# One dV quarter in front of each even unit's end product, and the gradient half first on ScalarE

## The chip, the cores and the metric

The kernel runs on one core of a Trainium2 chip. The core has five engines, each with an instruction queue of its own that is worked in order: TensorE (PE in the profile, with its weight loads shown as PEld), VectorE (DVE), ScalarE (ACT), GpSimd (POOL) and SyncE (SP, which here issues most of the DMA transfers). They meet through semaphores. TensorE writes its results to PSUM, an accumulator memory of eight banks; ScalarE and VectorE read them from there. The metric is the device time of one execution in microseconds, as the median of several runs. The profile is of one further execution.

## The reference

The kernel computes the output and all eight input gradients of two attention blocks side by side: A, a linear attention, and B, an ordinary softmax attention with 16 heads of 28 that share one key and one value head. The change is in B's main loop. Cut to that part:

```python
def _B_ref(x, wq, wk, wv, wo):          # x: 1 x 2048 x 448
    q = (x @ wq)                         # 16 heads of 28
    k, v = x @ wk, x @ wv                # one head of 28 each
    scores = einsum("bhqd,bkd->bhqk", q, k) * 28 ** -0.5
    p = softmax(scores)
    o = einsum("bhqk,bkd->bhqd", p, v)
    return o @ wo

def reference(..., grad_out):
    out, vjp = jax.vjp(f, A_x, A_wqkv, A_wo, B_x, B_wq, B_wk, B_wv, B_wo)
    return (out, *vjp(grad_out))
```

Going back through the softmax needs, for every head, query and key, the exponential of the score (E), the product of the output's gradient with the value (dP) and the product of both (dS). From these come o (from E and v), dq (from dS and k), dk (from dS and q) and dv (from E and the output's gradient).

## The kernel before

A first stage (about 185 us) does block A and prepares B: transposed q, k and v, each replicated into four groups of 32 partitions. The main loop then does B forwards and backwards, and a last stage (from about 1000 us) turns dq, dk and dv into the gradients of the weights and of x.

**Blocks and units.** The main loop runs over 64 blocks. A block is 256 queries and two heads (`blk`, L679). It is cut into 8 units, each of 256 keys: `u = 8 b + tp`, 512 units in all. A unit's work comes in stages that lie many units apart, so that one turn of the loop (L926) does, for the current u:

- scores of unit u (called S0 and S1 here, one for each of the two heads, "halves"): four matmuls, two key pieces of 128 for each half, on 32 rows of the array (`rows_SD`, L683);
- dP of unit w = u - 16 (D0 and D1), four matmuls in the same form in the same function. The four combinations use the array's four groups of 32 rows. The list `todo` (L687 to L689) gives their order;
- E of unit u on ScalarE: exp0 (L946) for half 0, exp1 (L992) for half 1, each 128 x 512;
- dS of unit w: half 0 on VectorE straight from PSUM (L958); half 1 by a copy on ScalarE (cp, L960) and a product on GpSimd (L961);
- in even units, the "end product" (`o_dq`, L889): o of units u-2 and u-1 and dq of the dS of units u-20 and u-19, 16 matmuls of 256 columns on four groups of 32 columns;
- in odd units, dk: 16 matmuls of 32 x 32 and 512 columns (`dk_m`, L860), from dS transposed by VectorE two units after dS was made (L1039);
- dv in four quarters a block (half h, query half qb; `dv_mm`, L896), each of four matmuls of 512 columns. It reads `eN`, E transposed by a DMA that SyncE issues behind exp1 of every fourth unit (L994), and `don`, the output's gradient divided by the softmax's sum. Before, the quarters stand in even units behind the end product: two when u modulo 8 is 4, one at 6, one at 2 (L1006 to L1008).

Beside these stand, once in a block: the copy of o from PSUM (L974, u modulo 8 = 1), the transposes of o (`onat_T`, L806, at 2) and its normalising (`o_norm`, L813), the copy of dq (L977, at 3), the row sums (`row_D`, at 4), the transposes of the gradient (`don_T`, L834, and `don_copy`, at 6), and from unit 32 a piece of an output projection (`do_proj`, `out_proj`, at 0; before unit 27 in odd units).

**Banks.** dP has two PSUM banks (`DB`), one for each half, used again in each unit: D0 of a unit may start when VectorE's product of the unit before has read its bank, D1 when cp of the unit before has. The scores turn over three banks (`SB`): S0 of u uses number 2u, S1 number 2u+1, modulo 3. So S1 takes the bank of S0 of the unit before, and the third, the "spare", is the bank of exp1 of the unit before and of the next unit's S0. In between it serves the transposes and projections.

**Order.** The order on each engine in the main loop is the order in which the code issues (`manual_schedule`, L917); nothing is moved by a scheduler. The lines that matter:

```python
            todo = [(0, 0), (0, 1), (1, 0), (1, 1)] * 2
            if sp is not None and dp is not None and u % 2 == 0:
                todo = [(0, 0), (0, 1), (1, 0)] * 2 + [(1, 1)] * 2
```

The first number is 0 for scores and 1 for dP, the second is the half.

Of the kernel before, what the change touches and what calls it, by code (L numbers as in the profile page):

```python
# [8 lines left out]
ACT = mybir.ActivationFunctionType  # L9
# [16 lines left out]
def kernel(  # L26
# [21 lines left out]
    nc = tc.nc  # L48
# [3 lines left out]
    scale = float(DH) ** -0.5  # L52
# [594 lines left out]
    NB = 64  # L647
# [3 lines left out]
    with ExitStack() as cs_:  # L651
# [17 lines left out]
        def eT(u):  # L669
            return ETs[u // 4 % 5][:, u % 4, :, :]  # L670

        def eN(b, c):
            return ENs[(2 * b + c // 2) % 6][:, 16 * (c % 2):16 * (c % 2) + 16, :]

        def mmt(out, lhsT, rhs, pos, start, stop):
            nc.tensor.matmul(out, lhsT=lhsT, rhs=rhs, start=start, stop=stop, tile_position=pos,  # L676
                             skip_group_check=True)

        def blk(b):  # L679
            qc, pair = divmod(b, 8)  # L680
            return qc, pair, pair // 2, pair % 2

        def rows_SD(u, sp, dp):  # L683
            b, tp = divmod(u, 8)
            w = u - 16
            qc, pair, g, hp = blk(b)
            todo = [(0, 0), (0, 1), (1, 0), (1, 1)] * 2  # L687
            if sp is not None and dp is not None and u % 2 == 0:
                todo = [(0, 0), (0, 1), (1, 0)] * 2 + [(1, 1)] * 2  # L689
            seen = {}  # L690
            for d in todo:
                if (dp if d[0] else sp) is None:
                    continue
                k, h = d
                t2 = seen.get(d, 0)
                seen[d] = 1
                t = 2 * tp + t2
                tc_ = slice(t * P, (t + 1) * P)
                oc = slice(t2 * 256, (t2 + 1) * 256)
                r = 64 * (1 - hp if k else hp) + 32 * h  # L700
                if k:
                    mmt(dp[h][:, oc], vT_rep[r:r + 32, tc_], doT[w // 8][r:r + 32, :], (r, 0), True, True)
                else:
                    mmt(sp[h][:, oc], kT_rep[r:r + 32, tc_], qT_B[g][r:r + 32, qc * 256:(qc + 1) * 256],
                        (r, 0), True, True)
# [96 lines left out]
        def due(u, lag):  # L802
            b, r = divmod(u - lag, 8)
            return b if r == 0 and 0 <= b < NB else None

        def onat_T(b, bank):  # L806
            onp = bank[:, 0:P].rearrange("p (q h c) -> p q h c", q=2, h=2)
            for qb in range(2):
                nc.tensor.transpose(onp[:, qb, :, :].rearrange("p h c -> p (h c)"), oTs[0:64, qb * P:(qb + 1) * P],  # L809
                                    identF[0:64, 0:64], tile_position=(0, 0))  # L810
            onps[b] = onp
# [48 lines left out]
        def dk_m(b, m, other=0):  # L860
            qc, pair, g, hp = blk(b)
            h, B, s = m // 8, (m // 2) % 4, m % 2
            for a in range(4):
                rhs = dsx[b][32 * a:32 * a + 32, :, h, :, :].rearrange(
                    "p u t (b i s) -> p u t b i s", b=4, s=2)[:, :, :, B, :, s]
                k = 32 * ((a + 2) % 4) if other else 32 * a
                mmt((dk_two if other else dk_acc)[k:k + 32, :],
                    qX[qc][32 * a:32 * a + 32, B, s, pair * 64 + 32 * h:pair * 64 + 32 * h + 32],
                    rhs, (32 * a, k), other == 2 or b == 0 and m == 0, other == 0 and b == NB - 1 and m == 15)
# [19 lines left out]
        def o_dq(vs, ys):  # L889
            for v, y in zip(vs, ys):  # L890
                todo = [f(i) for f, i in ((o_mm, v), (dq_mm, y)) if 0 <= i < NU]
                for _ in range(2):
                    for g_ in todo:
                        next(g_)

        def dv_mm(dv_acc, b, h, qb):  # L896
            for c in range(4):
                rhs = eN(b, c).rearrange("p (u h t q) k -> p u h t q k", u=2, h=2,
                                                       t=2)[:, :, h, :, qb, :]
                mmt(dv_acc[32 * c:32 * c + 32, :], don[b][:, qb, h, :], rhs, (0, 32 * c),  # L900
                    b == 0 and h + qb == 0, b == NB - 1 and h + qb == 2)
# [15 lines left out]
        with tc.manual_schedule():  # L917
# [8 lines left out]
            for u in range(NU + 28):  # L926
                w = u - 16
                hasS = u < NU
                hasD = 0 <= w < NU
                sp = [SB[(2 * u + h) % 3] for h in range(2)] if hasS else None  # L930
                dp = DB if hasD else None
                spare = SB[(2 * u + 2) % 3] if hasS else DB[u // 4 % 2] if u > 530 else SB[2]
                rows_SD(u, sp, dp)
                if (b := due(u, 10)) is not None:
                    onat_T(b, spare)
                if (b := due(u, 14)) is not None:
# [5 lines left out]
                    dps_ = DB[u // 2 % 2] if u < 16 else dk_acc if u < 27 else spare  # L942
                    do_proj(*dpj, dps_)

                if hasS:
                    nc.scalar.activation(out=eT(u)[:, 0, :], in_=sp[0][:, :], func=ACT.Exp, scale=scale)  # L946
                if u == 1:
                    q_shift(pn3, shifts[3], [pd_.tile([P, 2, 512], BF16, name="dsT").rearrange("p a b -> p (a b)").bitcast(F32)
                                             for _ in range(1)])
                    dv_acc = psA.tile([P, 512], F32, name="aacc")  # L950
# [3 lines left out]
                if hasD:  # L954
                    dst = pd_.tile([P, 2, 512], BF16, name="dsT")
                    dsT[w] = dst
                    ew = eT(w)
                    nc.vector.tensor_tensor(out=dst[:, 0, :], in0=dp[0][:, :], in1=ew[:, 0, :], op=ALU.mult)  # L958
                    cp = pc_.tile([P, 512], BF16, name="cp")
                    nc.scalar.activation(out=cp[:, :], in_=dp[1][:, :], func=ACT.Copy)  # L960
                    nc.gpsimd.tensor_tensor(out=dst[:, 1, :], in0=cp[:, :], in1=ew[:, 1, :], op=ALU.mult)  # L961
                gq, iq = divmod(u % 64 - 30, 8)
                qq = u // 64 + 1
                if 0 <= gq < 4 and u < 448:
# [34 lines left out]
                if u % 2:  # L999
                    b, i = divmod(u - 27, 8)  # L1000
                    if 0 <= b < NB:
                        for m in range(2 * i, 2 * i + 4):
                            dk_m(b, m, (1 + (u == 519 and m == 2 * i + 1)) * (m % 2) if 519 <= u < 537 else 0)
                else:
                    o_dq((u - 2, u - 1), (u - 20, u - 19))
                    b, n = divmod(u - 20, 8)  # L1006
                    for k in {0: (0, 1), 2: (2,), 6: (3,)}.get(n, ()) if 0 <= b < NB else ():
                        dv_mm(dv_acc, b, k // 2, k % 2)  # L1008
                y = u - 18

                if 512 <= u < 528 and u % 2 == 0:
# [10 lines left out]
                if u == 533:  # L1022
                    for c in range(4):
                        nc.scalar.activation(out=post["dkvT"][32:64, c * 512:(c + 1) * 512], in_=dv_acc[32 * c:32 * c + 32, :],
                                             func=ACT.Copy)
                if u == 536:
                    dk_sum = pd_.tile([P, 2, 512], BF16, name="dsT").rearrange("p a b -> p (a b)").bitcast(F32)
                    for c in range(2):
                        r = 64 * (1 - c)
                        nc.scalar.activation(out=dk_sum[64 * c:64 * c + 64, :], in_=dk_two[r:r + 64, :], func=ACT.Copy,  # L1030
                                             scale=scale)
# [3 lines left out]
                if 0 <= y < NU:  # L1035
                    b, tp = divmod(y, 8)
                    if tp == 0:
                        dsx[b] = px_.tile([P, 8, 2, 2, 256], BF16, name="dsx")
                    nc.vector.transpose(  # L1039
                        out=dsx[b][:, tp, :, :, :].rearrange("p h t c -> p (h t c)").bitcast(F32),  # L1040
                        in_=dsT[y][:, :, :].rearrange("p h c -> p (h c)").bitcast(F32))
# [67 lines left out]
        for c in range(4):  # L1109
            r = DC_ROWS[c]  # L1110
            ps = gen(0)
            for st in range(NS):
# [3 lines left out]
                                 func=ACT.Copy)  # L1116
# [35 lines left out]
```

## Time and profile before

| what | value |
|---|---|
| median of 3 runs | 1052.08 us (1051.96 to 1053.91) |
| the profiled execution's time | 1052.68 us |
| its span, first to last instruction | 1050.9 us |
| granted TensorE clock | 1.000 |
| busy share over the span: TensorE, VectorE, ScalarE, GpSimd | 96%, 85%, 83%, 76% |
| mean of one exp0, cp, exp1 | 612, 617, 629 ns |
| mean of one product on VectorE (L958), on GpSimd (L961) | 668, 1156 ns |
| mean of one transpose on VectorE (L1039) | 699 ns |
| median of one transfer eN<-eT on SyncE | 5376 ns, 128 of them |

Busy shares over the whole span mix the stages; the main loop's own share is read from a stretch in its middle. Instructions overlap at their ends, so the time between the starts of two ScalarE instructions is shorter than the duration of one. The end of a matmul is modelled by the profiler; its start is measured.

### The profile page before, as it was taken

The page shows a single profiled execution, that of the slowest core. Times are in us where ns is not written, and L with a number is a line of the kernel's source. Part 1 is how long each engine was busy: PE and PEld are TensorE (multiplying, and loading weights), DVE is VectorE, ACT ScalarE, POOL GpSimd, SP SyncE. Part 2 cuts the span into 40 slices and gives each one's busy share as a digit, 9 for nine tenths or more (in the row PEclk, how much of TensorE's full clock was granted, in tenths as well). Part 3 has the DMA queues.
Part 4 walks back from the last instruction along what each step waited for, and adds up shares of the span by engine and source line. Part 5 has one row for each costly group of instructions (what it writes and reads, how often), then busy time and mean ns, then how long its engine had stood idle before and what let it go on. Part 6 is the DMA issues. An engine that isn't in the chain of part 4 may idle for free.

```text
span 1050.9 us, 40033 instructions
## 1 busy us (share of the span) xinstructions
PE 1008.4 (96%) x16236; PEld 486.6 (46%) x16245; DVE 895.9 (85%) x1781; ACT 871.5 (83%) x1743; POOL 798.2 (76%) x1044
## 2 busy tenths in 40 slices
PE   9999999998999999999999999999999999999998
PEld 5555554434444444444444444444444444444444
DVE  6897500669999999999999999999999999999942
ACT  6463122589999999999999999999999999999632
POOL 8601272238888998899899989988998999888860
PEclk9999999999999999999999999999999999999999
DMA  9879999299999999999999999999999999999973
GB/s 266 150 134 192 189 222 215 42 163 202 188 196 190 188 195 198 194 193 191 197 175 195 192 202 185 204 199 184 192 194 191 194 190 193 204 186 182 220 156 87
DMA packets 689058, 195.15 MB, mean 186 GB/s; under 512 B 670408, under 2 KB 686688, under 8 KB 688872
## 3 DMA queue, kind: packets, MB, share of 16 engines
q1 hardware_dynamic: 680392, 179.97, 102.1%
q0 software_dynamic: 4544, 9.46, 3.4%
q10 hardware_dynamic: 3936, 3.16, 1.0%
q8 instruction: 127, 2.08, 0.8%
q14 instruction: 59, 0.48, 0.1%
HBM read 12.60 MB, written 10.84 MB: 22 GB/s over the span
## 4 chain that ended last, share of the span: by engine, by line
PE 44%; ACT 33%; issue 14%; DVE 6%; POOL 2%; DMA 0%; ACTq 0%; DVEq 0%; POOLq 0%
ACT cp L960 17%; ACT eT L992 13%; PE agen L81 13%; PE aacc L676 10%; PE agen L676 10%; PE aacc L81 6%; ACT eT L946 2%; DVE dsT L958 2%; PE aacc L809 2%; DVE dsx L1039 2%; PE aacc L840 1%; POOL dsT L961 1%; DMA out_dram<-dsT 0%; PE agen L313 0%; PE agen L227 0%
## 5 line engine op out<-in xcount | busy, mean ns | idle before, releaser
L961 POOL TENSOR_TENSOR dsT<-cp,eT 128x512 bf16<-128x512 bf16 x512 | 587.7, 1156 | 78.9 <-ACT cp L960 73.2
L1039 DVE STREAM_TRANSPOSE dsx<-dsT 128x512 f32<-128x512 f32 x512 | 357.8, 699 | 2.8 <-POOL dsT L961 0.7
L676 PEld LDWEIGHTS <-R 32*128 32x128 bf16 (+1 forms) x9104 | 228.5, 94 | 275.0 <-issue 239.4
L958 DVE TENSOR_TENSOR dsT<-agen,eT 128x512 bf16<-128x512 f32 x512 | 341.9, 668 | 10.6 <-PE agen L676 5.4
L960 ACT ACTIVATE cp<-agen 128x512 bf16<-128x512 f32 x512 | 315.8, 617 | 11.5 <-PE agen L676 10.5
L946 ACT ACTIVATE eT<-aacc 128x512 bf16<-128x512 f32 x512 | 313.6, 612 | 13.6 <-PE aacc L676 4.3
L992 ACT ACTIVATE eT<-aacc 128x512 bf16<-128x512 f32 x512 | 322.2, 629 | 0.0
L676 PE MATMUL agen<-dsx,qX 32*32 32x512 bf16 x4024 | 264.0, 376 | 0.0
L676 PE MATMUL agen<-doT,R 32*128 32x256 bf16 x2048 | 246.7, 269 | 4.2 <-DVE dsT L958 2.5
L676 PE MATMUL aacc<-R,R 32*128 32x256 bf16 (+1 forms) x2240 | 218.5, 269 | 7.1 <-DVE oTs L819 2.0
L676 PE MATMUL agen<-eT,R 128*32 128x256 bf16 x2048 | 157.4, 274 | 0.1
L676 PE MATMUL agen<-dsT,R 128*32 128x256 bf16 x2048 | 156.6, 274 | 0.1
L676 PEld LDWEIGHTS <-qX 32*32 32x32 bf16 x4096 | 78.2, 89 | 111.7 <-issue 53.3
L676 PE MATMUL aacc<-eN,don 128*32 128x512 bf16 x1024 | 96.7, 379 | 0.0
L81 PEld LDWEIGHTS <-R 128*128 128x128 bf16 x517 | 40.9, 98 | 42.2 <-issue 12.0
L81 PE MATMUL agen<-R,R 128*128 128x448 bf16 (+1 forms) x174 | 41.1, 360 | 1.8 <-ACT R L229 0.8
L851 POOL COPY qst<-R 128x512 bf16<-128x512 bf16 x56 | 34.2, 611 | 2.9 <-DMA qX<-qst 2.8
L823 POOL TENSOR_TENSOR prod<-R,oTs 128x128 f32<-128x128 bf16 x64 | 27.6, 431 | 9.3 <-DVE oTs L819 9.3
L676 PEld LDWEIGHTS <-don 128*32 128x32 bf16 x1024 | 33.8, 97 | 0.5
L586 DVE TENSOR_TENSOR osb<-R 32x512 bf16<-32x512 bf16 x4 | 1.7, 413 | 34.7 <-ACT R L583 34.7
L262 POOL TENSOR_SCALAR wdq<-wdq 128x448 bf16<-128x448 bf16 x16 | 21.1, 1327 | 12.9 <-DVE phiT L243 12.9
L427 POOL COPY pk<-R 128x256 bf16<-128x256 bf16 x4 | 1.6, 399 | 37.7 <-DVE R L389 37.7
(234 smaller groups left out, 983.1 us busy)
## 6 DMA issues: line engine op xcount, KB each, us to landing
eN<-eT SPq DMA_TRANSPOSE x128
xa<-in_A_x_dram SPq DMA_DIRECT2D x8, 224.0 KB
ga<-in_grad_out_dram SPq DMA_DIRECT2D x4, 448.0 KB
out_dram<-osb ACTq DMA_DIRECT2D x16, 112.0 KB
xa<-in_grad_out_dram POOLq DMA_DIRECT2D x4, 448.0 KB, 9.4
out_dram<-wdq POOLq DMA_DIRECT2D x8, 224.0 KB, 5.8
eT<-in_grad_out_dram SPq DMA_DIRECT2D x4, 448.0 KB
eT<-in_B_x_dram SPq DMA_DIRECT2D x4, 448.0 KB
```

What stands on the lines that cost most here:

```text
L81: nc.tensor.matmul(out_ap, lhsT=lhsT, rhs=rhs, start=start, stop=stop, tile_position=(0, 0))
L262: nc.gpsimd.tensor_scalar(out=wq_n[:, st, 0:D], in0=wq_n[:, st, 0:D], scalar1=1.0, scalar2=None, op0=ALU.min)
L676: nc.tensor.matmul(out, lhsT=lhsT, rhs=rhs, start=start, stop=stop, tile_position=pos, skip_group_check=True)
L809: nc.tensor.transpose(onp[:, qb, :, :].rearrange("p h c -> p (h c)"), oTs[0:64, qb * P:(qb + 1) * P], identF[0:64, 0:64], tile_position=(0 ...
L823: nc.gpsimd.tensor_tensor(out=prod[b][:], in0=dnv, in1=os_, op=ALU.mult)
L851: eng.tensor_copy(out=st.rearrange("p (b s) a j -> p b s a j", s=2)[:, :, s, :, :], in_=src.unsqueeze(2).to_broadcast([P, 4, 4, 32]))
L946: nc.scalar.activation(out=eT(u)[:, 0, :], in_=sp[0][:, :], func=ACT.Exp, scale=scale)
L958: nc.vector.tensor_tensor(out=dst[:, 0, :], in0=dp[0][:, :], in1=ew[:, 0, :], op=ALU.mult)
L960: nc.scalar.activation(out=cp[:, :], in_=dp[1][:, :], func=ACT.Copy)
L961: nc.gpsimd.tensor_tensor(out=dst[:, 1, :], in0=cp[:, :], in1=ew[:, 1, :], op=ALU.mult)
L992: nc.scalar.activation(out=eT(u)[:, 1, :], in_=sp[1][:, :], func=ACT.Exp, scale=scale)
L1039: nc.vector.transpose(out=dsx[b][:, tp, :, :, :].rearrange("p h t c -> p (h t c)").bitcast(F32), in_=dsT[y][:, :, :].rearrange("p h c -> p ...
```

## The change

Three things are moved; nothing is added or taken away.

1. The order of the eight matmuls of scores and dP becomes the same in every unit: D1, D0, S0, twice, then S1 twice.
2. On ScalarE, cp comes first in a unit, then exp0, then exp1 (before: exp0, cp, exp1).
3. Each even unit issues one dV quarter, just behind the scores and dP and in front of the transposes, the projections and the end product. A block's quarters come at units 18, 20, 22 and 24 after the block's first, in the order (0,0), (0,1), (1,0), (1,1) of half and query half; before, they came at 20 (two), 22 and 26, behind the end product.

```diff
-            todo = [(0, 0), (0, 1), (1, 0), (1, 1)] * 2
-            if sp is not None and dp is not None and u % 2 == 0:
-                todo = [(0, 0), (0, 1), (1, 0)] * 2 + [(1, 1)] * 2
+            todo = [(1, 1), (1, 0), (0, 0)] * 2 + [(0, 1)] * 2
...
                 rows_SD(u, sp, dp)
+                if u % 2 == 0:
+                    b, n = divmod(u - 18, 8)
+                    if 0 <= b < NB:
+                        dv_mm(dv_acc, b, n // 4, n // 2 % 2)
                 if (b := due(u, 10)) is not None:
                     onat_T(b, spare)
...
-                if hasS:
-                    nc.scalar.activation(out=eT(u)[:, 0, :], in_=sp[0][:, :], func=ACT.Exp, scale=scale)
...
                     cp = pc_.tile([P, 512], BF16, name="cp")
                     nc.scalar.activation(out=cp[:, :], in_=dp[1][:, :], func=ACT.Copy)
                     nc.gpsimd.tensor_tensor(out=dst[:, 1, :], in0=cp[:, :], in1=ew[:, 1, :], op=ALU.mult)
+                if hasS:
+                    nc.scalar.activation(out=eT(u)[:, 0, :], in_=sp[0][:, :], func=ACT.Exp, scale=scale)
...
                     o_dq((u - 2, u - 1), (u - 20, u - 19))
-                    b, n = divmod(u - 20, 8)
-                    for k in {0: (0, 1), 2: (2,), 6: (3,)}.get(n, ()) if 0 <= b < NB else ():
-                        dv_mm(dv_acc, b, k // 2, k % 2)
```

## The prediction

> **What bounds the kernel now.** I read the busy time by stretch first, then the chain of waits, then the timelines of ScalarE, TensorE, VectorE and SyncE around 602 to 611 us, where the main loop runs evenly.
>
> ```profile
> core 0: us, PE busy (x) PEld busy (x) DVE busy (x) ACT busy (x) POOL busy (x), PEclk, DMA share, GB/s
> 600.00:700.00 100.00, 96.68 (x1902) 45.30 (x1892) 97.93 (x191) 99.15 (x201) 90.25 (x110) 1.00 1.20 194
> ```
>
> Three engines are nearly full, ScalarE (ACT) most. 201 ScalarE instructions in 100 us are 67 units of three, so a unit takes 1.49 to 1.50 us.
>
> ```profile
> PE 44%; ACT 33%; issue 14%; DVE 6%; POOL 2%; DMA 0%; ACTq 0%; DVEq 0%; POOLq 0%
> ACT cp L960 17%; ACT eT L992 13%; PE agen L81 13%; PE aacc L676 10%; PE agen L676 10%; PE aacc L81 6%; ACT eT L946 2%; DVE dsT L958 2%; PE aacc L809 2%; DVE dsx L1039 2%; PE aacc L840 1%; POOL dsT L961 1%; DMA out_dram<-dsT 0%; PE agen L313 0%; PE agen L227 0%
> ```
>
> The chain alternates between the gradient copy (cp, L960), the second exponential (exp1, L992) and TensorE. So it is a loop between ScalarE and TensorE, seen here on ScalarE over two units:
>
> ```profile
> 603.04 0.60 ACT L960 ACTIVATE cp<-agen 128x512 bf16<-128x512 f32 x1
> 603.52 0.62 ACT L992 ACTIVATE eT<-aacc 128x512 bf16<-128x512 f32 x1
> 603.99 0.63 ACT L946 ACTIVATE eT<-aacc 128x512 bf16<-128x512 f32 x1
> 604.47 0.65 ACT L960 ACTIVATE cp<-agen 128x512 bf16<-128x512 f32 x1
> 604.95 0.66 ACT L992 ACTIVATE eT<-aacc 128x512 bf16<-128x512 f32 x1
> 605.49 0.61 ACT L946 ACTIVATE eT<-aacc 128x512 bf16<-128x512 f32 x1
> ```
>
> Without a wait, starts are 1.91/4 = 0.478 us apart, so three need 1.434. The last step took 0.54, because the first exponential (exp0, L946) waited. The same stretch on TensorE:
>
> ```profile
> 604.55 0.39 PE L676 MATMUL aacc<-R,R 32*128 32x256 bf16 x2
> 604.73 0.26 PE L676 MATMUL agen<-doT,R 32*128 32x256 bf16 x1
> 605.17 0.26 PE L676 MATMUL agen<-doT,R 32*128 32x256 bf16 x1 [0.18 <-ACT cp L960]
> 605.17 0.28 PE L676 MATMUL aacc<-R,R 32*128 32x256 bf16 x2
> 605.18 0.36 PE L676 MATMUL agen<-doT,R 32*128 32x256 bf16 x2
> 605.47 1.04 PE L676 MATMUL agen<-dsx,qX 32*32 32x512 bf16 x16
> 606.45 0.28 PE L676 MATMUL aacc<-R,R 32*128 32x256 bf16 x2
> ```
>
> In an odd unit gradient half 1 (D1) stands fourth. It writes the bank that cp of the unit before must have read: cp began at 604.47, D1 at 605.17, 0.70 later. Behind D1 stand the second score pieces, and exp0 began 0.32 after the release. My tally of ScalarE's timeline over units 264 to 447, as mean times from one exp0 to the next by unit modulo 8: 1.50, 1.45, 1.70, 1.45, 1.53, 1.45, 1.51, 1.45, or 12.03 us a block of eight. The lost time lies in the steps that start at an even unit; the 1.70 is the block with the output transposes.
>
> **The change, part by part.** No engine gets or loses an instruction, so the sum is one of waits.
>
> ScalarE order cp, exp0, exp1; D1 first on TensorE. Let cp(even) begin at 0. It frees D1(odd) at 0.70, long before cp(odd), which is due at 1.43. TensorE must start the odd unit's first D1 by 1.43 - 0.43 = 1.00: the second D1 stands 0.12 behind (rows 603.51 and 603.63) and a matmul reaches ScalarE 0.31 after its start (605.17 to 605.49). So that wait goes. What is late next is S1, now last: it needs the bank of the even unit's exp0, which begins at 0.48, so S1 begins at 0.48 + 0.70 = 1.18. The dK product is queued behind it, 0.30 later (605.17 to 605.47), and takes 0.98 to the next scores (605.47 to 606.45); then D1 to cp 0.43. The loop from cp to cp over two units: 1.18 + 0.30 + 0.98 + 0.43 = 2.89. ScalarE alone needs 2 x 1.434 = 2.87. I take 2.88, against 2.94 now for the plainest pair (602.55 to 605.49).
>
> dV quarter in front of the end product. Four column tiles take 0.22 (598.46: eight last 0.60; 601.72 alike: four last 0.38). The total of four a block is unchanged. The place is new: before, the output transposes (L809), gradient transposes (L840) and projections wait behind the scores for the bank of exp1 of the unit before (21.5 us before L809 alone from 300 to 950 us). With S1(even) released at 1.18 - 1.43 = -0.25, the scores end about 0.05; exp1, begun at -0.48, frees its bank at 0.22. The dV quarter fills 0.05 to 0.27, so it costs nothing there; without that cover it would cost 4 x 0.22 = 0.88 a block. Plain pair: 0.27 + 0.55 (end product, 604.00 to 604.55) = 0.82, before the 1.00 allowed. Projection, 0.19 more: 1.01, just in time. Output transposes: the next tile shape begins 0.32 after the last dV quarter starts (second four of the eight at 598.68, scores at 599.00), then 0.26 (607.13 to 607.39), then 0.55: scores from 1.18. VectorE's normalising must also leave the spare bank, about 1.27 by its rows (0.19 + 0.29 + 0.05 after the transposes, which land near 0.74). Then the second D1 is at 1.28, cp(odd) at 1.59, dK at 1.69, and the pair takes 1.69 + 0.98 + 0.43 = 3.10, against 1.70 + 1.45 = 3.15.
>
> Block: 3 x 2.88 + 3.10 = 11.74, against 12.03; 0.29 x 60 blocks (units 32 to 511) = 17.4 us gained.
>
> Ramp, units 0 to 15, scores only: S0, S0, S1, S1 in place of alternating pairs. Two pieces of one half start 0.11 apart (603.63 and its successors), so up to 0.1 a unit on a TensorE that there sets the pace: 0 to +1.6, I take +1.5. Tail, units 512 on, gradient halves only, alternating as before: 0.
>
> SyncE's transposes eN<-eT. They are issued as before, after exp1, but their queue is close behind:
>
> ```profile
> 647.30 11.28 SPq L994 DMA_TRANSPOSE eN<-eT  x2
> 658.63 1.30 SPq L855 DMA_TRANSPOSE qX<-qst  x1
> 660.04 10.66 SPq L994 DMA_TRANSPOSE eN<-eT  x2
> ```
>
> Where a block also moves qX, the queue needs 12.6 us for eight units (647.30 to 660.04 is 12.74, the next 12.50); elsewhere 10.8 (seven eN in 37.38). Over 128 units, with the 3.4 us transpose of the outputs (599.28), that is 8 x 12.6 + 8 x 10.8 + 3.5 = 190.7, or 1.49 a unit; the new pace is 11.74/8 = 1.468. So the queue falls behind 0.022 x 416 = 9 us by unit 448. Now 10 units, not 12, lie between the last transpose of a block and the first dV that reads it: 14.7 - 5.4 (one eN) - 2.1 (the landing of eN's other transfers) = 7.2 of lag are free, and about 3 are in use. 9 - 4 = 5 us would be given back; blocks that find the queue idle have shorter transposes (4.9 against 5.4), so I take 3, between 0 and 9.
>
> Sum: -17.4 + 1.5 + 3 = -13 on the span of 1050.9, which is 1052.7 for that execution; it lies 0.6 above the median, within 0.1%. So 1039.8; I say 1040. Bounds: ScalarE never waiting in the plain pairs and no lag paid, about 1030; half the gain per block and 9 us of lag, 1052.
>
> **The rivals.**
>
> A. SyncE's queue sets the pace from early on. For: it is back to back through every qX stretch. Against: it had 7 us of lag to spare before dV needs it. 416 units at 1.49 in place of the 627 us that they take now: -7; last eight blocks -2.3, ramp +1.5: 1045.
>
> B. Slower: VectorE's product (L958) holds TensorE. D0 is second in line now, and it needs the bank that this product reads; behind D0 stand both scores, the second D1 and with it cp.
>
> ```profile
> 607.09 0.65 DVE L958 TENSOR_TENSOR dsT<-agen,eT 128x512 bf16<-128x512 f32 x1
> 610.46 0.69 DVE L958 TENSOR_TENSOR dsT<-agen,eT 128x512 bf16<-128x512 f32 x1
> ```
>
> For: the pair with the normalising costs VectorE 3.37 here against 3.10 for the rest. The others need 2.97, 2.63 and 2.62 by their rows (product to product 1.22 a unit, 0.2 to 0.33 an extra), 11.6 of 11.74 in all. Today a D0 already waits (0.28 behind its score, 599.00 to 599.30). Against: D0 may come 1.09 after cp(even) (1.43 - 0.31 - 0.03) and the next cp is still on time; the product begins near 0.05, frees the bank 0.70 later, and with a lag of 0.34 (3.37 + 0.07 for its wait on the transposes, less 3.10) that is 1.09. If the 0.34 of lag and one such 0.28 are paid each block: 12.36, +20 us: 1073. It decides from 0.29 a block.
>
> C. TensorE's own work sets the pace, and S1, last and alone, makes it longer: an undisturbed four-wide odd phase takes 0.33 (608.21 to 608.54), the new order 0.43, 0.40 a block; with 0.1 for one more change of tile shape and less 0.24 for even units (0.49 now, 603.51 to 604.00) that is +0.26 x 60 = +16: 1068. For: 96.7% busy. Against: matmul ends are modelled, and TensorE stands still 0.44 between 604.73 and 605.17. The Trainium skill ("TensorE: Matmul & The Clock Gate", section "Why this matters for your kernels") speaks for this rival: small-K matmuls gain by running concurrently in distinct row groups, and the new order takes S1 out of that company. The trace agrees on the form (four starts within 0.02 us), which alone doesn't say that TensorE sets the pace.
>
> D. The change moves the wait from exp0 to exp1 or cp and nothing is gained: 1052.
>
> **How the numbers follow.** Forecast 0.56 (its own range 1030 to 1047), A 0.2, D 0.08, B 0.12, C 0.04. The time is the forecast's, 1040. Down to 1030 and up to 1053 leaves out B and C and a little at either end, near 2 in 10. About 0.2%, 2 us, is what a measurement here can tell from no change. Faster: 0.56 + 0.2 = 0.76; same 0.08; slower 0.16.
>
> **What would show it.** Right: exp1 to cp and cp to exp0 near 0.48 in nearly every unit, steps from even units near 1.44 but for the one with output transposes; S1 in odd units starting right after exp0 ends; the wait before L809 gone; SyncE's transposes back to back with a growing lag after each exp1. Wrong: D0 waiting for L958 with cp late behind it (B), TensorE without any wait on ScalarE (C), dV waiting on a transfer (A), steps of 1.50 and above at even units.

## The result, and the profile after

The changed kernel is slower: median 1059.47 us over four runs (1058.11 to 1059.88) against 1052.99 before (1051.96 to 1054.50), a ratio of 1.0059 [1.0046, 1.0071]. Its profiled execution took 1059.88 us with a span of 1058.2, 7.3 more than before. The forecast of 1040 and its whole range were missed.

The busy time in the same even stretch of the main loop (columns as in the prediction):

```profile
core 0: us, PE busy (x) PEld busy (x) DVE busy (x) ACT busy (x) POOL busy (x), PEclk, DMA share, GB/s
600.00:700.00 100.00, 98.22 (x1875) 44.67 (x1875) 96.87 (x188) 98.03 (x198) 89.86 (x110) 1.00 1.22 196
```

ScalarE does 198 instructions in this stretch, not 201, and TensorE is the fuller by 1.5 points. TensorE has no more work than before, and it starts fewer matmuls in this stretch (1875, not 1902). So the busy time counted for one matmul grew, and not the work. The chain of waits says what stands in the way:

```profile
PE 62%; DVE 23%; POOL 6%; issue 4%; ACT 3%; DMA 1%; DVEq 0%; ACTq 0%; POOLq 0%
PE agen L676 30%; PE agen L81 13%; PE aacc L676 11%; DVE dsT L958 9%; DVE dsx L1038 8%; PE aacc L81 6%; POOL dsT L961 3%; ACT cp L960 2%; DVE R L979 1%; POOL prod L821 1%; POOL don L824 1%; DVE oTs L817 1%; DVE oTs L976 1%; POOL R L825 1%; DVE rl L816 1%
```

ScalarE fell from 33% of the chain to 3%, so the change did what it says: the wait of the first exponential behind a held D1 is gone. VectorE rose from 6% to 23%, with its product (L958) and its transpose (L1038, L1039 before) at the front. The waits for one instruction between 300 and 900 us (total us, times, longest) show the same from TensorE's side:

```profile
PEld aacc L807 <- ACT eT L994: 11.1, 49, 0.2
PE agen L676 <- DVE dsT L958: 6.3, 25, 0.3
```

The wait in front of the output transposes fell from 19.9 to 11.1 us in that window; the dV quarter fills it, for it is 19.9 again in e1 below, where the quarter is back in its old place. The wait of D0 for VectorE's product is new; before, no such line of L676 stands there. The profile names it 25 times in these 50 blocks. This is how it looks in the timeline, over units 4 and 5 of a block and then from unit 7 to unit 0 of the next:

```profile
601.76 0.62 ACT L960 ACTIVATE cp<-agen 128x512 bf16<-128x512 f32 x1
...
602.30 0.69 DVE L958 TENSOR_TENSOR dsT<-agen,eT 128x512 bf16<-128x512 f32 x1
...
602.52 0.28 PE L676 MATMUL agen<-doT,R 32*128 32x256 bf16 x1
...
603.04 0.26 PE L676 MATMUL agen<-doT,R 32*128 32x256 bf16 x1 [0.25 <-DVE dsT L958]
...
603.05 0.28 PE L676 MATMUL agen<-doT,R 32*128 32x256 bf16 x1
...
603.43 0.60 ACT L960 ACTIVATE cp<-agen 128x512 bf16<-128x512 f32 x1
...
607.27 0.68 ACT L994 ACTIVATE eT<-aacc 128x512 bf16<-128x512 f32 x1
...
607.44 0.27 PE L676 MATMUL agen<-doT,R 32*128 32x256 bf16 x2
...
607.81 0.63 ACT L960 ACTIVATE cp<-agen 128x512 bf16<-128x512 f32 x1
```

First part: the product starts 0.54 after cp. D1 starts at 602.52, D0 stands second and can't start before 603.04, 0.74 after the product's start; the second D1 and so the next cp come behind it. The step from cp to cp is 1.67, not 1.43. Second part: a plain pair. The second D1 starts at 607.44 and cp at 607.81, 0.37 later; exp1 had begun at 607.27, so a free ScalarE would have taken cp at 607.75.

My tally of ScalarE's timeline says where the whole difference lies. It gives the mean time from the first ScalarE instruction of a unit to that of the next, for units 144 to 447, by unit modulo 8, in us:

| pair of units | before | predicted | after | after less predicted |
|---|---|---|---|---|
| 0, 1 (plain) | 2.947 | 2.88 | 2.956 | 0.08 |
| 2, 3 (output transposes, normalising) | 3.151 | 3.10 | 3.197 | 0.10 |
| 4, 5 | 2.986 | 2.88 | 3.058 | 0.18 |
| 6, 7 | 2.956 | 2.88 | 2.942 | 0.06 |
| block | 12.04 | 11.74 | 12.155 | 0.415 |

By stretches of units, counted in the same way, the span changed so: units 0 to 15 +2.75 us, 16 to 47 -1.31, 48 to 447 +5.33, 448 to 503 +0.64, the rest -0.20; together 7.21.

### The profile page after: what moved, and what is told of

Read it like the earlier page. It is cut to its first block, busy times and chain, and to the rows that moved or that the text cites. A ratio compares the mean times of both kernels' runs of the same rounds, so it can differ in the third digit from the quotient of the medians.

```text
span 1058.2 us, 40025 instructions
## 1 busy us (share of the span) xinstructions
PE 1030.8 (97%) x16236; PEld 486.8 (46%) x16245; DVE 896.6 (85%) x1781; ACT 872.7 (82%) x1743; POOL 799.9 (76%) x1044
## 4 chain that ended last, share of the span: by engine, by line
PE 62%; DVE 23%; POOL 6%; issue 4%; ACT 3%; DMA 1%; DVEq 0%; ACTq 0%; POOLq 0%
PE agen L676 30%; PE agen L81 13%; PE aacc L676 11%; DVE dsT L958 9%; DVE dsx L1038 8%; PE aacc L81 6%; POOL dsT L961 3%; ACT cp L960 2%; DVE R L979 1%; POOL prod L821 1%; POOL don L824 1%; DVE oTs L817 1%; DVE oTs L976 1%; POOL R L825 1%; DVE rl L816 1%
## 5 line engine op out<-in xcount | busy, mean ns | idle before, releaser
L676 PEld LDWEIGHTS <-R 32*128 32x128 bf16 (+1 forms) x9104 | 246.3, 94 | 253.9 <-issue 204.3
L1038 DVE STREAM_TRANSPOSE dsx<-dsT 128x512 f32<-128x512 f32 x512 | 356.8, 697 | 2.3 <-DVE doT L845 0.2
L958 DVE TENSOR_TENSOR dsT<-agen,eT 128x512 bf16<-128x512 f32 x512 | 338.8, 662 | 13.5 <-PE aacc L676 6.8
L676 PE MATMUL agen<-dsx,qX 32*32 32x512 bf16 x4024 | 264.0, 376 | 0.0
L676 PE MATMUL aacc<-R,R 32*128 32x256 bf16 (+1 forms) x2240 | 260.0, 264 | 1.8 <-ACT eT L963 0.6
L676 PE MATMUL agen<-doT,R 32*128 32x256 bf16 x2048 | 232.6, 273 | 14.9 <-DVE dsT L958 9.4
L676 PE MATMUL agen<-eT,R 128*32 128x256 bf16 x2048 | 155.8, 274 | 0.4 <-DMA wo<-wo_d 0.4
L676 PE MATMUL agen<-dsT,R 128*32 128x256 bf16 x2048 | 155.6, 273 | 0.1
L676 PEld LDWEIGHTS <-qX 32*32 32x32 bf16 x4096 | 78.4, 89 | 112.9 <-issue 54.6
L676 PE MATMUL aacc<-eN,don 128*32 128x512 bf16 x1024 | 102.3, 390 | 0.0
L676 PEld LDWEIGHTS <-don 128*32 128x32 bf16 x1024 | 26.2, 92 | 53.8 <-issue 53.8
L821 POOL TENSOR_TENSOR prod<-R,oTs 128x128 f32<-128x128 bf16 x64 | 27.5, 430 | 11.2 <-DVE oTs L817 11.1
```

Source lines behind the costliest of these rows:

```text
L821: nc.gpsimd.tensor_tensor(out=prod[b][:], in0=dnv, in1=os_, op=ALU.mult)
L1038: nc.vector.transpose(out=dsx[b][:, tp, :, :, :].rearrange("p h t c -> p (h t c)").bitcast(F32), in_=dsT[y][:, :, :].rearrange("p h c -> p ...
```

## The experiments

All ratios are to the kernel before, measured beside it on the same chip, with 95% intervals; 4 to 12 runs each. The medians are of several sessions, in which the kernel before took 1053.25 us (e1 to e5), 1053.13 (e7 to e10) and 1053.48 (e11 to e13), so compare ratios. The steps are my tally of the one profiled execution, as means over units 144 to 447.

| kernel | median us | ratio | units 0,1 | 2,3 | 4,5 | 6,7 | block |
|---|---|---|---|---|---|---|---|
| before | 1052.99 | 1 | 2.947 | 3.151 | 2.986 | 2.956 | 12.038 |
| after | 1059.47 | 1.0059 [1.0046, 1.0071] | 2.956 | 3.197 | 3.058 | 2.942 | 12.155 |
| e1, order alone | 1056.18 | 1.0037 [1.0025, 1.0050] | 2.940 | 3.178 | 2.984 | 3.019 | 12.121 |
| e2, dV place alone | 1055.66 | 1.0025 [1.0015, 1.0036] | 2.948 | 3.215 | 2.984 | 2.961 | 12.106 |
| e3, D0 further back | 1055.00 | 1.0019 [1.0009, 1.0029] | 2.950 | 3.156 | 3.055 | 2.946 | 12.107 |
| e5, no dq copy | 1051.80 | 0.9989 [0.9979, 0.9999] | 2.957 | 3.189 | 2.924 | 2.968 | 12.037 |
| e7, cp with one wait | 1053.51 | 1.0005 [0.9996, 1.0014] | 2.924 | 3.176 | 3.062 | 2.905 | 12.066 |
| e8, one dV quarter back | 1054.88 | 1.0012 [1.0003, 1.0021] | 2.957 | 3.208 | 2.986 | 2.950 | 12.099 |
| e9, before with dq copy on ScalarE | 1067.71 | 1.0137 [1.0122, 1.0153] | 2.952 | 3.486 | 2.927 | 2.940 | 12.306 |
| e10: e11, with dq copy on ScalarE | 1066.27 | 1.0125 [1.0111, 1.0139] | 2.951 | 3.545 | 2.865 | 2.939 | 12.300 |
| e11, e3 and e7 and e8 | 1051.08 | 0.9976 [0.9966, 0.9986] | 2.955 | 3.168 | 2.996 | 2.933 | 12.052 |
| e12, e1 and e7 | 1052.43 | 0.9989 [0.9980, 0.9999] | 2.905 | 3.191 | 2.994 | 2.969 | 12.058 |
| e13, before, D1 last always | 1053.43 | 1.0002 [0.9993, 1.0010] | 2.887 | 3.181 | 2.971 | 2.976 | 12.017 |

### The two halves of the change: e1 and e2

e1 is the changed kernel with the dV quarters in their old place; e2 is the kernel before with only the dV quarters moved, the same edit the other way round. The edit of e1:

```diff
-                if u % 2 == 0:
-                    b, n = divmod(u - 18, 8)
-                    if 0 <= b < NB:
-                        dv_mm(dv_acc, b, n // 4, n // 2 % 2)
...
                     o_dq((u - 2, u - 1), (u - 20, u - 19))
+                    b, n = divmod(u - 20, 8)
+                    for k in {0: (0, 1), 2: (2,), 6: (3,)}.get(n, ()) if 0 <= b < NB else ():
+                        dv_mm(dv_acc, b, k // 2, k % 2)
```

> The changed kernel with the four dV quarters back behind the end product, where they stood before; the new order of matmuls and of ScalarE stays. Theory T (the order is at fault: D0, second in line, waits for VectorE's product, and S0, third, for the normalising in the spare bank, and cp stands behind both): still slower than before, ratio 1.004 to 1.009, with the step from the unit with modulo 4 at 1.60 us or more. Rival R1 (the place of dV is at fault: it delays the output transposes and so the normalising): at or below before, ratio 0.990 to 1.001. Rival R2 (dV, two units earlier, waits for eN): as R1.

> The kernel before with only the dV quarters moved in front. T: 0.995 to 1.001, since the quarter fills a time in which TensorE waits for exp1. R1: 1.004 to 1.010. R2: 1.003 or more, with TensorE waiting on a DMA at dV.

Each half alone costs time, 0.37% and 0.25%. That these add up to about the 0.59% of both says little, for they lie in different pairs: e1 loses 0.063 in units 6 and 7 and 0.027 in 2 and 3, e2 0.064 in 2 and 3, and the changed kernel 0.072 in 4 and 5 and 0.046 in 2 and 3.

Theory T named a step of 1.60 from the units with modulo 4 as its sign in e1. It is 1.530, so the order alone doesn't make the hold of units 4 and 5. In units 6 and 7 of e1 the dV quarter stands behind the end product again, where nothing covers it, and the second D1 of unit 7 starts 1.18 after cp of unit 6; in the changed kernel, with the quarter in front, it is 1.02 (medians). So in that pair the quarter in front lies under a wait, as the prediction had it.

In e2, whose ratio lies between what T and R1 forecast, the whole difference is in units 2 and 3: the medians of the timeline there say that the output transposes start 0.34 after the unit's first ScalarE instruction, not 0.20, and VectorE's normalising ends at 1.29, not 1.22. No wait of TensorE for a transfer stands among e2's waits from 300 to 900 us, which speaks against R2. The wait of D0 for the product does stand there (5.6 us, 25 times), yet units 4 and 5 lose nothing (2.984): in the old order cp comes later in the unit, so the late D0 holds nothing up. Of e2's chain of waits VectorE now has the largest part:

```profile
DVE 43%; PE 33%; POOL 10%; issue 8%; ACT 5%; DVEq 0%; POOLq 0%; ACTq 0%
```

### Is it VectorE's lag? e5

The changed kernel without VectorE's copy of dq (L979); the copy is left out, so the gradients that are made from dq are not delivered.

```diff
-                if (b := due(u, 27)) is not None:
-                    qc, pair, g, hp = blk(b)
-                    nc.vector.tensor_scalar(out=qT_B[g][64 * hp:64 * hp + 64, qc * 256:(qc + 1) * 256],
-                                            in0=oq[64:128, 0:256], scalar1=scale, scalar2=None, op0=ALU.mult)
```

> The changed kernel without VectorE's copy of dq out of PSUM (one 0.43 us copy a block, in the unit with modulo 3; dq is then not delivered). T: VectorE's lag at the product of modulo 4 goes from 0.47 to 0.2 us or less after cp, the step from modulo 4 from 1.61 to 1.50 or less, ratio about 0.994 to 1.000. If VectorE's load has no part in it: 1.004 to 1.007 as the changed kernel, with the step from modulo 4 unchanged.

The block falls by 0.118 to 12.037 and the time to 0.9989 [0.9979, 0.9999]. In units 4 and 5 the pair falls from 3.058 to 2.924; the product there starts 0.07 before cp, where it stood 0.47 behind it (means). The same place of another block, from e5's timeline:

```profile
645.91 0.69 DVE L958 TENSOR_TENSOR dsT<-agen,eT 128x512 bf16<-128x512 f32 x1
645.97 0.62 ACT L960 ACTIVATE cp<-agen 128x512 bf16<-128x512 f32 x1
...
646.85 0.27 PE L676 MATMUL agen<-doT,R 32*128 32x256 bf16 x2
...
647.40 0.66 ACT L960 ACTIVATE cp<-agen 128x512 bf16<-128x512 f32 x1
```

The second D1 and D0 start within 0.01 of each other (the x2), with no wait, and cp follows cp by 1.43, ScalarE's own pace. So one VectorE instruction of 0.43 us a block, which neither TensorE nor ScalarE waits for there, sets that pair. It also frees the bank of dq for the next end product, but that is not what e5 gains: in the changed kernel the copy ends 0.23 before the first cp of unit 4 and the end product starts 0.27 after it (medians). Two kernels with the copy in place agree: in e1 and e8, with the same order, the product stands 0.39 behind cp and the pair takes 2.984 and 2.986.

### Can the order let D0 come late? e3

```diff
-            todo = [(1, 1), (1, 0), (0, 0)] * 2 + [(0, 1)] * 2
+            todo = [(1, 1)] * 2 + [(0, 0)] * 2 + [(1, 0), (0, 1)] * 2
```

> The changed kernel with the order D1, D1, S0, S0, D0, S1, D0, S1: both D1 stand in front of everything that waits for VectorE, so cp waits for neither the product nor the normalising; D0 comes with S1, which has to wait for exp0 anyway. T: the steps from modulo 2 and 4 fall from 1.75 and 1.61 to 1.55 or less, a block to 11.6 to 11.9 us, ratio 0.982 to 0.994. R1 and R2: nothing gained over the changed kernel, 1.003 to 1.008.

A miss for T, which forecast 0.982 to 0.994: the hold doesn't go, it moves by one unit. The step from unit 4 falls from 1.608 to 1.446, that from unit 5 rises from 1.450 to 1.609; the pair stays (3.055). The timeline of e3 shows how:

```profile
646.14 0.69 DVE L958 TENSOR_TENSOR dsT<-agen,eT 128x512 bf16<-128x512 f32 x1
...
646.39 0.27 PE L676 MATMUL agen<-doT,R 32*128 32x256 bf16 x1
...
646.89 0.26 PE L676 MATMUL agen<-doT,R 32*128 32x256 bf16 x1 [0.23 <-DVE dsT L958]
...
646.99 0.62 ACT L960 ACTIVATE cp<-agen 128x512 bf16<-128x512 f32 x1
...
647.21 1.05 PE L676 MATMUL agen<-dsx,qX 32*32 32x512 bf16 x16
...
648.31 0.27 PE L676 MATMUL agen<-doT,R 32*128 32x256 bf16 x1
...
648.67 0.60 ACT L960 ACTIVATE cp<-agen 128x512 bf16<-128x512 f32 x1
```

Both D1 are out by 646.39 and cp is in time at 646.99, but D0 starts at 646.89, 0.75 after the product, the dK product stands behind it, and the next D1 behind that: 1.68 to the next cp. The gain over the changed kernel (1.0019 against 1.0059) lies, by the profiles, in units 2 and 3 (3.156 against 3.197), and in the ramp, where e3's profile has 1.5 us less (the last section says why).

### What makes the plain pair longer than its sum? e7

cp waits for two engines: for D1 on TensorE, and for GpSimd, which must have read cp's buffer. A second condition stands in an instruction of its own in front of cp. e7 moves the wait for GpSimd onto exp1 of the unit before, so that cp waits for TensorE alone; nothing else changes.

```diff
-                    nc.scalar.activation(out=cp[:, :], in_=dp[1][:, :], func=ACT.Copy)
-                    nc.gpsimd.tensor_tensor(out=dst[:, 1, :], in0=cp[:, :], in1=ew[:, 1, :], op=ALU.mult)
+                    cpi = nc.scalar.activation(out=cp[:, :], in_=dp[1][:, :], func=ACT.Copy)
+                    pool_ins[u] = (cpi.ins, nc.gpsimd.tensor_tensor(out=dst[:, 1, :], ...).ins)
...
-                    nc.scalar.activation(out=eT(u)[:, 1, :], in_=sp[1][:, :], func=ACT.Exp, scale=scale)
+                    x1 = nc.scalar.activation(out=eT(u)[:, 1, :], in_=sp[1][:, :], func=ACT.Exp, scale=scale)
+                    for ins in pool_ins.get(u - 2, ()):
+                        tc.add_manual_dep(x1.ins, ins.name, ...)
```

> The changed kernel, with the wait for GpSimd (that the cp buffer is free again) moved from cp to exp1 of the unit before, so that cp waits for TensorE alone and by itself; before, its wait for TensorE stood in a separate semaphore instruction in front. Theory W (that separate wait makes a cp that truly waits start 0.06 us later than an exp0 does): cp starts 0.31 after the second D1 in place of 0.37, steps of 1.48 to 1.50 fall to 1.43 to 1.46, a block loses 0.1 to 0.25 us, ratio 0.994 to 1.002. Rival (the delay belongs to D1 or to the loop, not to the form of the wait): the release stays at 0.37, ratio 1.004 to 1.008.

The instructions of cp's line, the first from the changed kernel, the second from e7:

```profile
L960 ACTq EVENT_SEMAPHORE  x510: 17/17/435, 229.3 to 1010.5; - x170
```

```profile
L961 ACTq EVENT_SEMAPHORE  x16: 17/17/437, 227.1 to 1003.2; - x16
```

510 separate waits became 16. Where cp had waited, it began 0.36 after the start of the last gradient matmul in the changed kernel (median of 128 cases, and 0.36 in e1) and 0.30 in e7 (98 cases; 0.30 in e12). In a plain pair of e7:

```profile
605.69 0.27 PE L676 MATMUL agen<-doT,R 32*128 32x256 bf16 x2
...
606.00 0.69 ACT L961 ACTIVATE cp<-agen 128x512 bf16<-128x512 f32 x1
```

0.31, against 0.37 above. The block falls by 0.089, a little less than the 0.1 to 0.25 that theory W forecast, the plain pairs by 0.03 and 0.04, and the kernel is level with before: 1.0005 [0.9996, 1.0014]. Units 4 and 5 gain nothing (3.062), since there cp waits behind D0 and so for VectorE. The Trainium skill ("Perfetto Trace Analysis", section "Identifying Dependency Chains") says that an instruction which waits for several engines may get separate semaphore instructions in front of it; the 510 rows agree, and the 0.06 us is what this case measures for it.

### The dV quarter of the pair with the normalising: e8

```diff
-                    if 0 <= b < NB:
+                    if 0 <= b < NB and n:
                         dv_mm(dv_acc, b, n // 4, n // 2 % 2)
...
                     o_dq((u - 2, u - 1), (u - 20, u - 19))
+                    b, n = divmod(u - 18, 8)
+                    if n == 0 and 0 <= b < NB:
+                        dv_mm(dv_acc, b, 0, 0)
```

> The changed kernel with one of the four dV quarters, that of the unit with modulo 2 (where the outputs are transposed), behind the end product; the other three stay in front. Theory (the whole cost of the new place is the delay of the transposes and the normalising in that unit): the step from modulo 2 falls by 0.05 to 0.07 us, ratio 1.002 to 1.005. Rival (dV in front costs in the other units too, or by waiting for eN): step unchanged elsewhere than there by less than 0.03, ratio 1.005 to 1.008.

One quarter put back behind the end product makes the block 0.056 shorter. The output transposes start at 0.20 again, and the product of unit 4 stands 0.39 behind cp, not 0.47. But the gain is not where theory and rival looked for it: units 2 and 3 stay (3.208), for the second D1 of unit 3 starts at 1.35 in both kernels (medians), and units 4 and 5 fall from 3.058 to 2.986. So what the quarter costs in front goes through VectorE's lag, two units later.

### Was the hold of the old order the cost? e13

The kernel before with its order of even units, D1 last, in odd units too, so that exp0 no longer waits for scores behind a held D1.

```diff
-            if sp is not None and dp is not None and u % 2 == 0:
+            if sp is not None and dp is not None:
                 todo = [(0, 0), (0, 1), (1, 0)] * 2 + [(1, 1)] * 2
```

> The kernel before with the order of its even units in the odd ones too (S0, S1, D0, twice, then D1 twice), so that the second score piece of an odd unit no longer stands behind a D1 that waits for cp. If that hold on exp0 is what the plain pairs of the kernel before lose: steps from modulo 0 and 6 fall from 1.50 to 1.45, ratio 0.992 to 0.998. If the loop cp, D1, dK, next scores (0.70 + 0.30 + 0.98 and on) sets the pair anyway, as the same loop through S1 does in the changed kernel: the loss moves to the next step, 0.998 to 1.003.

The pair 0, 1 falls to 2.887, which is ScalarE's pace, but units 2, 3 and 6, 7 take 0.05 of the 0.06 back, and the time is the same: 1.0002 [0.9993, 1.0010]. The wait that the prediction set out to remove is real and can be removed, yet it is not what limits a block.

### The dq copy moved to ScalarE: e9 and e10

e9 is the kernel before, e10 is e11 (below), each with the dq copy as a ScalarE instruction at the head of the unit.

```diff
-                    nc.vector.tensor_scalar(out=qT_B[g][64 * hp:64 * hp + 64, qc * 256:(qc + 1) * 256],
-                                            in0=oq[64:128, 0:256], scalar1=scale, scalar2=None, op0=ALU.mult)
...
                 spare = SB[(2 * u + 2) % 3] if hasS else DB[u // 4 % 2] if u > 530 else SB[2]
+                if (b := due(u, 27)) is not None:
+                    qc, pair, g, hp = blk(b)
+                    nc.scalar.activation(out=qT_B[g][64 * hp:64 * hp + 64, qc * 256:(qc + 1) * 256],
+                                         in_=oq[64:128, 0:256], func=ACT.Copy, scale=scale)
```

> The kernel before with the dq copy of the unit with modulo 3 moved from VectorE to ScalarE, in front of that unit's exp0, where ScalarE stands idle for about 0.29 us. Theory V (VectorE's lag from the normalising to the product of modulo 4 sets the pace of that half of the block in the kernel before too): the lag of the product at modulo 4 falls from 0.46 to 0.2 or less, the step from 1.54 to 1.47 or less, ratio 0.988 to 0.997. Rival (it is TensorE's work that sets it): 0.999 or more.

> The changed kernel with the order D1, D1, S0, S0, D0, S1, D0, S1, cp's single wait, the dV quarter of modulo 2 behind the end product, and the dq copy on ScalarE. If the three costs named (VectorE's lag, the form of the wait, the delayed transposes) are what took the gain: a block of 11.6 to 11.85 us, ratio 0.975 to 0.992. If SyncE's queue or the loop through S1 and dK holds the pace anyway: 0.993 or more.

A miss: 1.4% and 1.3% slower. VectorE's lag does go (the product of unit 4 stands 0.36 ahead in e9, and units 4, 5 fall to 2.927 and 2.865), but the copy must wait for the end product, and at the head of ScalarE's queue everything waits with it. From e9's timeline of ScalarE:

```profile
601.53 0.64 ACT L992 ACTIVATE eT<-aacc 128x512 bf16<-128x512 f32 x1
602.20 0.38 ACT L935 ACTIVATE R<-agen 64x256 bf16<-64x256 f32 x1
602.60 0.60 ACT L950 ACTIVATE eT<-aacc 128x512 bf16<-128x512 f32 x1
```

From exp1 to the next exp0 1.07, where 0.48 is the pace. A copy placed later in ScalarE's queue was not tried.

### Repaired versions: e11 and e12

e11 is the changed kernel with the edits of e3, e7 and e8; e12 is e1 with that of e7, that is, the new order with one wait for cp and dV in its old place.

> The changed kernel with three of the repairs together: the order D1, D1, S0, S0, D0, S1, D0, S1; cp's wait for TensorE by itself; the dV quarter of modulo 2 behind the end product. If the three costs add up (0.05, 0.09 and 0.06 us a block off 12.155): 11.95 us a block, ratio 0.993 to 0.999. If they are one and the same cover (VectorE's sequence from the normalising to the product of modulo 4 holds whatever the order): 12.05 or more, 1.000 to 1.003.

> The changed kernel with the dV quarters in their old place and cp's wait by itself: the new order alone, without the price of the separate wait. If the wait is what made the order alone dearer than before (12.12 against 12.04 us a block): 12.03 us or less, ratio 0.997 to 1.001. If it is S1, last and held by exp0, with dK behind it: steps from odd units stay at 1.46 to 1.49, 1.002 to 1.005.

e11 beats both kernels, at 0.9976 [0.9966, 0.9986], and e12 is a little faster than before, at 0.9989 [0.9980, 0.9999]. e11's ratio fits the first forecast, its mean block of 12.052 the second. The mean hides what happens: by the median, the blocks of its profiled execution take 12.00 and 11.89 by turns, before 12.03 and 11.97, which is 0.055 less a block, or about 3 us in 60 blocks. Two blocks of 13.2 and 13.3 us (from units 304 and 424) raise the mean, and this execution, at 1053.46, is the longest of its ten. In both blocks GpSimd waits for a transfer, 1.90 and 2.04 us. A line of the waits from 300 to 900 us names it:

```profile
POOL qst L849 <- DMA qX<-qst: 8.6, 8, 2.0
```

GpSimd waits 8.6 us for transfers qX in SyncE's queue, in 8 places, and not at all in the changed kernel; the longest lag of a transpose behind the end of its exp1 is 6.9 us there, 5.0 in the changed kernel, 4.6 before. e12 has the same pattern (6.7 us in 8 places, a block of 13.1 us from unit 304).

## Why the prediction was wrong

**The loop was the right one, and it was removed.** ScalarE left the chain, and in the plain pairs S1 starts 0.68 behind exp0, where 0.70 was forecast. But the forecast sized the loops that took the old one's place too small, and the one that B warned of had no slack at all.

**"Then D1 to cp 0.43": mis-sized.** It is 0.12 between two D1 and 0.31 from a matmul to ScalarE, and the 0.31 was taken from exp0. cp has a second condition, and begins 0.36 to 0.37 after its matmul, so the term is 0.48. The other terms of that loop came as forecast in the plain pairs (medians: exp0 at 0.48 to 0.49, S1 0.68 behind it, dK 0.30, the next D1 0.98). With 0.48 the prediction's own sum is 2.94, and 2.94 to 2.96 was measured; that is all that was to be gained there. e7 takes the second wait away and gets half of it, 0.03 and 0.04 a pair; S1 then starts 0.74 to 0.76 behind exp0, and why it does stays open.

**"With a lag of 0.34 (3.37 + 0.07 ...)" and "that is 1.09": mis-sized, and rival B with it.** The sum allowed D0 to come 1.09 after cp and reckoned 1.09, so that it held only if nothing was too small. D0 came at 1.21: the product of unit 2 already stands 0.10 behind cp, not 0.05; VectorE's pair with the normalising, of which the 3.37 was one block, takes 3.56 (3.45 before), beside a pair of units of 3.20, which makes the lag 0.47; and D0 starts 0.74 behind the product, not 0.70 (means). So B's wait is there: the second D1 and cp stand behind D0, cp of unit 5 comes 1.61 after that of unit 4, ScalarE needs its 1.45 for the next step, and units 4 and 5 take 3.058 where 2.88 was forecast. e5 takes VectorE's copy away and gets 0.134 of these 0.178 back; about 0.04 is left, near the 0.06 to 0.08 that plain pairs lose. B's mechanism was right as it was written, with D0 second in line and cp behind it; its price of 0.62 a block was too high, since the lag is made good by unit 6 (0.03), and its chance of 0.12 looks low.

**"So it costs nothing there": the dV quarter.** For TensorE's own chain it was nearly right. What it moves is the output transposes, by 0.14, and with them VectorE's normalising, by 0.07, on an engine that doesn't make it good before unit 4. e2 prices the move at 0.064 a block in the old order, e8 that of the one quarter at 0.056 in the new. The prediction did see the normalising end later, at about 1.27 (1.29 was measured), but charged that to the spare bank alone and not to VectorE's sequence.

**Output transposes pair, 3.10: the wrong path.** 3.197 was measured, where it was 3.151 before. By the medians the scores begin 0.05 behind the end of the normalising, the second D1 at 1.35, not 1.28, and cp of unit 3 0.37 behind that, at 1.72, not 1.59. From there ScalarE needs 1.45: 3.17 (3.197 by the means, with cp at 1.75). The prediction went on along TensorE instead, where its 1.69 and 0.98 came true, and with 0.48 for the last term that path is 3.15. This reading is from the timeline of one execution; no run takes this delay away by itself (3.176 with one wait for cp, 3.156 with D0 further back).

**The ramp, +1.5,** was right: in the profiles without the dip in the clock (last section) units 0 to 15 took 1.2 to 1.3 more (e1, e3, e7). Units 16 to 47 gave back 1.0 to 1.7 of it. The changed kernel's own +2.75 has the dip in it. **The tail, 0,** was right too: -0.1 from unit 504 on in the changed kernel.

**SyncE's queue, +3.** It was worked out from a pace of 1.468 a unit, under the queue's 1.49. The pace became 1.52, the lag did not build up (at most 5.0 us, before 4.6), and rival A had no say. Waits for the queue's transfers show in the faster kernels, 8.6 us in e11, but also 2.4 and 2.5 in e1 and e2, so that the pace alone doesn't explain them.

**C** (TensorE's own work) is not what sets units 4 and 5: e5 takes nothing from TensorE and the time falls. **D**, the wait that merely changes place, is near the truth for the plain pairs.

The error of a block, 0.415, is thus 0.08 and 0.06 in the plain pairs, 0.10 with the output transposes, and 0.18 in units 4 and 5, each rounded.

## What to carry to other kernels

Here three engines were over 96% busy, and removing the wait that the chain showed handed the bound to the next loop, a few hundredths away. In such a stage, work out the next two loops with medians over many periods, and take as suspect any slack under 0.1 us that rests on one row; a sum that comes out equal to what it is allowed has no slack. Price the start of an instruction from rows of that same instruction: cp, which waited on two engines, started 0.06 us later than with one wait. And follow a moved piece of work to the engine that consumes what now comes later, even where the piece itself lies under cover.

## What the runs showed of the hardware

The second wait made cp start 0.06 us later (e7 above), though the row of that wait lasts only 17 ns.

TensorE's granted clock fell to half for 3.4 us early in the main loop of the changed kernel's profiled execution. Busy time and granted clock of four microseconds there, first before, then after:

```profile
210.00:214.00 4.00, 3.92 (x35) 1.68 (x36) 3.21 (x6) 3.71 (x8) 1.32 (x2) 1.00 1.04 189
```

```profile
206.00:210.00 4.00, 3.31 (x45) 1.68 (x42) 3.40 (x7) 2.52 (x6) 2.35 (x6) 1.00 0.36 113
210.00:214.00 4.00, 3.63 (x20) 1.14 (x20) 2.53 (x5) 2.33 (x5) 1.24 (x2) 0.57 1.04 191
```

20 matmuls instead of 35, and ScalarE at 5 instructions instead of 8. Such an execution can be told by its mean clock of 0.998. It came in 28 of 81 runs of the nine kernels that put D1 first on TensorE, and in none of 96 runs of the four with the old order or nearly so (before, e2, e9, e13); within a kernel these runs are 1.0 to 2.6 us longer by the median, and the profiles with the dip have 1.4 to 1.5 us more in units 0 to 15 than those without. 28/81 of the 1.0 to 2.6 us is 0.3 to 0.9 us on the average run, which no count of waits would give. The Trainium skill ("TensorE: Matmul & The Clock Gate", section "What's actually happening") describes a gate that passes either half or all of the clock, by a free-running window of 3.4 us in which activity is watched; the half and the 3.4 us agree. The Trainium skill puts the half down to an idle window. In the 3.41 us right in front of the dip (207.19 to 210.60) TensorE was busy for 2.40 us, and in the kernel before for 2.57 in the corresponding 3.41 us (207.40 to 210.81), without a dip behind them. So the window was not idle, and what exactly sets the dip off stays open.
